# A state-space attention and MoE kernel: hand-ordered schedule replaced by a searched step list, with four operations moved to other engines

## The chip, the cores and the metric

The kernel runs on one core of one Trainium2 chip. The metric is the device time in microseconds (us) of one execution. A core has five engines that run their own instruction queues in order: TensorE (PE; its weight loads, PEld, overlap its matmuls), VectorE (DVE), ScalarE (ACT), GpSimd (POOL) and SyncE (SP), which here only issues transfers. Sixteen DMA engines move data between HBM and the on-chip memory.

## The reference, cut to what matters

```python
# attention, per batch b (4) and head h (8), 768 steps, head size 48
for t in range(S):
    cur = einsum('bhd,bhe->bhde', u * k[t], v[t])
    y[t] = einsum('bhd,bhde->bhe', r[t], state + cur)
    state = w[t][..., None] * state + einsum('bhd,bhe->bhde', k[t], v[t])
x = y.transpose(0, 2, 1, 3).reshape(3072, 384)      # tokens x (heads * size)
out = gelu_tanh(x @ w_in) @ w_out                   # 384 -> 2048 -> 384
```

Both kernels cut the tokens into 12 units: three windows of 256 tokens for each of four batches. A unit goes through attention (decay sums `z`, `x`; scaled operands `kk`, `rq`; their transposes `T`; scores `mt`; output `y`; state product `p`), then a transpose of its 256x384 result, then the MoE part: `h` (48 matmuls), GELU `g`, and `o` (32 matmuls).

## The kernel before

Weights arrive as fp32 on SyncE's queue and three engines convert them. Operand transposes are on PE for the first three units and on the DMA after that. Scores are masked by a product; the `u` diagonal is added apart.

```python
def load_w_in(i):
    t = pstage.tile([P, DF // 2], FP, tag=f"wi{i}", name=f"wi{i}")
    SP.dma_start(out=t, in_=moe_w_in[ts(cb, P), ts(hf, DF // 2)])
def cast_w_in(i, eng):
    cast(eng, w_in_sb[:, cb, ts(hf, DF // 2)], stages.pop(("i", i)))
...
PE_T = (3, 3)
def a2(q, which):
    if q < PE_T[which]:                       # units 0 to 2: PE, then a copy by VectorE
        ...
        return
    for c2 in range(2):                       # units 3 to 11: two DMA transposes
        SP.dma_start(out=..., in_=src[...], transpose=True)
...
    a6(0)                                     # x of unit 0 is ready
    cast_w_in(0, ACT)
    cast_w_in(1, ACT)
    att = attention(1)
    ...
    table("gelu")
    for i in range(8):
        mm1(0, i)                             # all of h of unit 0
        if i in (0, 2, 4, 5, 6, 7):
            next(att)                         # attention of unit 1 in between
    table("exp")                              # only now: decays of unit 2
    ww(2)
    ln(2)
    mm2(0, 0, range(6))
    a1(2)
    exps(2)
```

ScalarE loads a function table before it changes between logarithm or exponential on one side and GELU on the other (25 loads of 1.28 us in this trace).

## Time and profile before

| what | value |
|---|---|
| time, median of 3 (range) | 201.08 us (201.01 to 201.49) |
| PE busy in the profiled run | 179.5 of 202.0 us |

The profile's main lines are shown in the prediction.

### The profile page before, as it was taken

The page shows a single profiled execution, that of the slowest core. Times are in us where ns is not written, and L with a number is a line of the kernel's source. Part 1 is how long each engine was busy: PE and PEld are TensorE (multiplying, and loading weights), DVE is VectorE, ACT ScalarE, POOL GpSimd, SP SyncE. Part 2 cuts the span into 40 slices and gives each one's busy share as a digit, 9 for nine tenths or more (in the row PEclk, how much of TensorE's full clock was granted, in tenths as well). Part 3 has the DMA queues.
Part 4 walks back from the last instruction along what each step waited for, and adds up shares of the span by engine and source line. Part 5 has one row for each costly group of instructions (what it writes and reads, how often), then busy time and mean ns, then how long its engine had stood idle before and what let it go on. Part 6 is the DMA issues. An engine that isn't in the chain of part 4 may idle for free.

```text
span 202.0 us, 5310 instructions
## 1 busy us (share of the span) xinstructions
PE 179.5 (89%) x2200; PEld 126.4 (63%) x2200; DVE 132.7 (66%) x238; ACT 117.0 (58%) x188; POOL 124.3 (62%) x126
## 2 busy tenths in 40 slices
PE   3867499599998796999999999999989999999991
PEld 1245167485676564866767767677567677776760
DVE  7499874529888585548486697797397677374011
ACT  2226647876474483568585665674584757456650
POOL 3999683595985995895892993964967910000000
PEclk9998569999999999999999999999999999999997
DMA  6999999999559967878969959769879564301102
GB/s 160 258 270 334 394 301 332 221 272 251 142 80 211 242 121 177 208 99 198 225 119 251 156 95 259 151 134 279 121 169 209 92 118 69 80 3 35 46 9 68
DMA packets 76552, 35.15 MB, mean 174 GB/s; under 512 B 70512, under 2 KB 75760, under 8 KB 76528
## 3 DMA queue, kind: packets, MB, share of 16 engines
q1 hardware_dynamic: 76528, 34.81, 78.1%
q8 instruction: 17, 0.28, 0.7%
q14 instruction: 7, 0.06, 0.1%
HBM read 25.36 MB, written 4.72 MB: 149 GB/s over the span
## 4 chain that ended last, share of the span: by engine, by line
PE 58%; DMA 9%; DVE 4%; ACT 4%; SPq 3%; issue 2%; POOL 2%; ACTq 0%; POOLq 0%
PE h L393 24%; PE o L402 22%; DMA TT<-rq 7%; SPq L272 3%; PE mt L285 3%; PE y L308 2%; DMA TT<-kk 2%; PE cum L181 2%; PE y L356 2%; PE p L331 2%; PE xTp L378 1%; ACT L163 1%; DVE rq L244 1%; DVE kk L244 1%; POOL rk L206 1%
## 5 line engine op out<-in xcount | busy, mean ns | idle before, releaser
L395 ACT ACTIVATE g<-h 128x512 bf16<-128x512 f32 x96 | 56.8, 597 | 52.1 <-PE h L393 50.9
L393 PE MATMUL h<-xT,w_in_sb 128*128 128x256 bf16 x576 | 76.9, 277 | 5.2 <-DVE w_in_sb L86 2.2
L402 PE MATMUL o<-w_out_sb,g 128*128 128x384 bf16 x384 | 72.5, 326 | 0.5 <-DVE w_out_sb L86 0.5
L393 PEld LDWEIGHTS <-w_in_sb 128*128 128x128 bf16 x576 | 54.1, 99 | 18.5 <-issue 5.3
L402 PEld LDWEIGHTS <-g 128*128 128x128 bf16 x384 | 36.6, 98 | 18.8 <-issue 0.7
L291 DVE TENSOR_TENSOR mtsb<-mt,mask 128x512 bf16<-128x512 f32 x48 | 29.9, 683 | 5.3 <-PE mt L285 5.2
L216 POOL TENSOR_TENSOR vsc<-vb,dg 128x768 bf16<-128x768 bf16 x12 | 17.9, 1490 | 9.9 <-DVE dg L215 7.3
L215 DVE TENSOR_REDUCE dg<-rk 128x16 f32<-128x768 f32 x12 | 11.4, 948 | 17.7 <-POOL rk L206 17.7
L410 DVE COPY ob<-o 128x384 f32<-128x384 f32 x24 | 13.2, 551 | 14.2 <-PE o L402 13.8
L206 POOL TENSOR_TENSOR rk<-rk,r 128x768 f32<-128x768 f32 x12 | 21.7, 1809 | 0.9
L202 POOL TENSOR_TENSOR rk<-k,u_bc 128x768 f32<-128x768 f32 x12 | 21.7, 1812 | 0.1
L256 POOL TENSOR_TENSOR am<-blk,al 128x384 f32<-128x384 bf16 x24 | 20.2, 860 | 0.0
L163 ACT ACT_TABLE_LOAD x13 | 16.7, 1283 | 0.9 <-PEq L645 0.7
L194 POOL TENSOR_TENSOR kw<-k,w 128x384 f32<-128x384 f32 x9 | 9.0, 999 | 12.7 <-DMA k<-in_k_dram 12.7
L345 DVE TENSOR_TENSOR p<-p,S 128x384 f32<-128x384 f32 x16 | 9.1, 567 | 9.9 <-PE p L331 9.1
L165 ACT ACT_TABLE_LOAD x12 | 15.4, 1283 | 0.2
L168 ACT ACTIVATE logw<-ww 128x384 bf16<-128x384 f32 x12 | 6.2, 523 | 14.8 <-POOL ww L173 10.4
L195 POOL TENSOR_TENSOR rw<-r,w 128x384 f32<-128x384 f32 x10 | 10.3, 1032 | 5.7 <-DMA r<-in_r_dram 5.7
L364 DVE TENSOR_TENSOR xs<-y,vsc 64x384 bf16<-64x384 f32 x24 | 13.3, 554 | 0.7
L285 PE MATMUL mt<-TT,TT 48*64 48x128 bf16 x384 | 10.1, 227 | 3.3 <-DMA TT<-rq 2.4
L346 DVE TENSOR_TENSOR S<-p,am 128x384 bf16<-128x384 f32 x20 | 11.1, 557 | 2.6 <-PE p L331 1.9
L285 PEld LDWEIGHTS <-TT 48*64 48x64 bf16 x384 | 6.8, 110 | 7.4 <-issue 7.2
(68 smaller groups left out, 189.6 us busy)
## 6 DMA issues: line engine op xcount, KB each, us to landing
w<-in_w_dram SPq DMA_DIRECT2D x12, 384.0 KB, 6.1
k<-in_k_dram SPq DMA_DIRECT2D x12, 384.0 KB, 5.4
r<-in_r_dram SPq DMA_DIRECT2D x12, 384.0 KB, 5.8
v<-in_v_dram SPq DMA_DIRECT2D x12, 384.0 KB, 6.5
out_dram<-ob SPq DMA_DIRECT2D x48, 96.0 KB, 2.3
wi<-in_moe_w_in_dram SPq DMA_DIRECT2D x6, 512.0 KB, 8.8
wo<-in_moe_w_out_dram SPq DMA_DIRECT2D x8, 384.0 KB, 5.8
TT<-kk SPq DMA_TRANSPOSE x18, 3.6
```

The lines of the kernel that those rows point to most:

```text
L163: ACT.preload_act_table_set(EXP_SET)
L165: ACT.preload_act_table(AF.Gelu_apprx_tanh)
L202: POOL.tensor_tensor(out=rk, in0=kt.rearrange("p h (t d) -> p h t d", t=2), in1=u_bc[:, :, None, :].broadcast_to([P, H, 2, D]), op=AL.mult)
L206: POOL.tensor_tensor(out=rk, in0=rk, in1=rt.rearrange("p h (t d) -> p h t d", t=2), op=AL.mult)
L216: POOL.tensor_tensor(out=vsc, in0=vb, in1=dg.rearrange("p h t -> p t h")[:, :, :, None].broadcast_to([P, 2, H, D]), op=AL.mult)
L256: POOL.tensor_tensor(out=st["am", q][:, c2], in0=blk.rearrange("p g j d -> p g (j d)"), in1=st["al", q][:, :, c2][:, :, None].broadcast_to ...
L285: PE.matmul(mts[j][ds(64 * c2, 64), gi, t2, :], kT[ds(64 * j, D), c2, g, t2, :], rT[ds(64 * j, D), c2, g, :, :], start=(gi + t2 == 0), sto ...
L291: DVE.tensor_tensor(out=sb[:, j], in0=mts[j], in1=mask.rearrange("p a b t -> p a (b t)")[:, None, :, :].broadcast_to([P, 2, 2, P]), op=AL. ...
L364: DVE.tensor_tensor(out=st["xs", q][rows, c2, :].rearrange("p (h d) -> p h d", h=H), in0=ys[c2][rows, :, :], in1=st["vsc", q][ds(64 * c2, ...
L393: PE.matmul(h[:, f, :], w_in_sb[:, cb, ts(ft, P)], xT[:, :, cb, :], start=(f + cb == 0), stop=(cb == NCB - 1), skip_group_check=True)
L395: ACT.activation(out=st["g", q][:, ds(2 * i, 2), :], in_=h, func=AF.Gelu_apprx_tanh)
L402: PE.matmul(st["o", q, c2], g[:, ft, ts(c2, P)], w_out_sb[:, ft, :], start=(ft == 0), stop=(ft == NFT - 1))
```

## The change

The intent is to keep PE full. A list of some 1,000 steps, found by search, fixes the order on every engine and the PSUM bank of every result. With it come these parts (core of the diff, cuts marked "..."):

```diff
+ORDER = """
+const.3.D load.w.0.0 const.2.D load_u.A clr.sc.2.P clr.lwl.0.D load.w.0.1 clr.rq.1.P lnL.0.0
+...
+cum.2@7 Xc.0.A sel.1 a5.1.1 xd.2@1 clr.lw.1.P xs.1.0.A ez.2 xs.1.1.A mm1.0.3@3 sm.0.1
+..."""
-        SP.dma_start(out=t, in_=moe_w_in[ts(cb, P), ts(hf, DF // 2)])
-        cast(eng, w_in_sb[:, cb, ts(hf, DF // 2)], stages.pop(("i", i)))
+        POOL.dma_start(out=w_in_sb[i],                       # fp32 to bf16 on the way
+                       in_=moe_w_in[:, ts(i, sz)].rearrange("(c p) f -> p c f", p=P))
...
-            DVE.tensor_tensor(out=sb[:, j], in0=mts[j], in1=mask..., op=AL.mult)
+        POOL.tensor_tensor(out=<diagonal of sc>, in0=eye..., in1=d..., op=AL.mult)     # dI
+        DVE.copy_predicated(sc..., mask..., st["mt", q, n][j]...)                      # mk
...
-        for dst, tri in ((x, strict), (z, incl)):
-            PE.matmul(dst[:, 0:HD], tri, lw[:, :, 0:D], start=True, stop=True)
+        PE.matmul(z[:, 0:HD], incl, lw[:, :, 0:D], start=True, stop=True)
+        DVE.tensor_tensor(out=x..., in0=z..., in1=logws[q % NLW][:, :, 0:D], op=AL.subtract)
...
-            PE.transpose(ps[:, c2, cb, :], xs[:, c2, ts(cb, P)], ident)   # all units
+        SP.dma_start(out=st["xT", q][:, c2], in_=..., transpose=True)     # Xd, units 6 to 11
...
+            ACT.activation(out=t.rearrange("p f (c i s) -> p (f c) s i", c=2, s=2),
+                           in_=h.rearrange("p f (c s i) -> p (f c) s i", c=2, s=2),
+                           func=AF.Gelu_apprx_tanh)                       # for those units
...
-            POOL.tensor_tensor(out=st["am", q][:, c2], in0=blk..., in1=al..., op=AL.mult)
+    (state updates read the decay directly, in halves of 64 partitions, on VectorE)
```

Operand transposes stay on PE for units 0 to 4 and for one operand of unit 5. In the step list, `mm1.0.3@3` is chunk 3 of `h` of unit 0 into bank 3, and a last letter names the engine. Attention of units 0 and 1 now comes before any `h`, and 44 small dummy matmuls (`warm`) stand in the gaps.

## The prediction

> **What bounds the kernel now.** I read the page's busy shares and slices first, then the costliest groups, then the chain of work that ended last, then the busy times of the first 50 us in stretches of 5 us.
>
> ```profile
> span 202.0 us, 5310 instructions
> PE 179.5 (89%) x2200; PEld 126.4 (63%) x2200; DVE 132.7 (66%) x238; ACT 117.0 (58%) x188; POOL 124.3 (62%) x126
> ...
> PE   3867499599998796999999999999989999999991
> PEclk9998569999999999999999999999999999999997
> DMA  6999999999559967878969959769879564301102
> ```
>
> TensorE is the fullest engine, and the other three have a third of the span free. But the tenth-filled slices show two regimes: nine slices of start-up (45 us) with holes and a dip of the clock, then a nearly full PE.
>
> ```profile
> 160.84 1.31 PE h L393 x12
> 162.15 0.57 PE mt L285 x32
> ...
> 165.31 0.51 PE y L308 x32
> 165.81 0.34 PE p L331 x8
> ...
> 170.19 0.34 PE xTp L378 x6
> 170.52 3.25 PE o L402 x20
> 173.77 1.31 PE h L393 x12
> ```
>
> This is the chain (start, length, what) over one undisturbed unit (one of 12 windows of 256 tokens): 173.77 - 160.84 = 12.93 us, all PE. It gives the true cost of each kind of matmul when they follow one another, which the group means (277 ns for `h`) hide because those overlap: `h` (first MoE product) 1.31/12 = 0.109 us each, 48 a unit, 5.25 us; `o` (second product) 3.25/20 = 0.1625, 32 a unit, 5.20 us; scores `mt` 0.57; `y` 0.51; `p` 0.34; from other rows of the same chain the state product 0.17 for each half (0.34), the x transposes 0.34, the decay sums 0.40 (0.33 for the two of 384 columns), 16 kk/rq transposes 0.89 (0.445 for one operand), four diagonal matmuls (`sel`) 0.33.
>
> Useful PE work before: 12 x (5.25 + 5.20 + 0.57 + 0.51 + 0.34 + 0.34) = 146.5, less 4 x 0.17 = 0.7 for the state products that four first halves don't have, plus transposes of x 4.1, sums 4.8, 6 operand transposes 2.7, `sel` for six units 2.0: **159.4 us**. So 202.0 - 159.4 = 42.6 us of the span is not useful PE work. It splits so: at 40.21 us the PE has done about 14.9 us of it (units 0 and 1 of attention, one unit and a quarter of `h`, eight `o`): 25.3 us lost. From 40.2 to the last matmul's end at 197.6 us there are 157.4 us for the remaining 144.5: 12.9 lost. From there the last eviction and store take 4.4.
>
> ```profile
> 20.00:25.00 5.00, 2.05 (x12) 1.00 (x10) 4.54 (x5) 3.69 (x4) 3.50 (x2) 0.50 1.02 403
> 35.00:40.00 5.00, 3.03 (x24) 1.94 (x23) 2.84 (x7) 4.25 (x7) 2.25 (x3) 1.00 0.93 223
> ```
>
> (PE, PEld, DVE, ACT, POOL busy, granted clock, DMA share, GB/s.) MoE starts at 20.4 us but gets no further: PE is 2.05 of 5 us busy at half clock, waiting for weights that VectorE, ScalarE and GpSimd convert (2.3, 1.06 and 1.5 us for 128x1024). At 35 to 40 us it waits for converted output weights, tables and gelu. The later loss is mostly this:
>
> ```profile
> 58.77 0.57 SPq L272
> 59.39 2.84 DMA TT<-rq
> ```
>
> a DMA transpose of the scores' operand, issued behind other DMAs, with the PE waiting.
>
> **What the Trainium skill says.** "TensorE: Matmul & The Clock Gate", Part 1 (the HAM clock gate): a PE idle over a window of about 3.4 us drops to half clock, and a busy window restores it. The trace agrees roughly: after 10 to 20 us at 70% modelled busy with gaps, the clock is 0.50 and 0.60 in the two next stretches. "DMA: Bandwidth & Descriptors", SWDGE vs HWDGE vs iDMA: a cast during DMA needs GpSimd's software descriptors, so the new weight loads must be issued from there. The kernel before has none; no run shows its rate yet. The same page, Queues, rings and completion order: each DMA engine goes round its queues by packet, so GpSimd's weights will share with SP's inputs instead of standing behind them. The trace before has nearly everything on one queue, so doesn't show it. "TensorE: Matmul & The Clock Gate", Weight-path perf modes: fast weight load wants 128 columns, not fp32, with a column step of -1,023 to 1,024 elements; the new step of 4 is inside. No weight load before is strided, so the trace doesn't show this either.
>
> **The change part by part.**
>
> *Weights.* The six `wi` and eight `wo` loads with staging, and 14 casts (6 for w_in 8.5 us, 8 for w_out 5.3 us over three engines) go. Six converting DMAs take their place. Off the steady path, on the start-up path. Bytes read don't change: 12 x 1.57 MB inputs and 6.3 MB weights. Inputs ran at 209 GB/s in the first 10 us, weights at up to 403. Two units of inputs (3.15 MB) cost about 15 us of DMA, all weights 16, two more units 15: 48 us with the 2 us of first landing, against PE's need of all of it at about 50 us. Tight, but no wall.
>
> *Order.* Attention of units 0 and 1 now goes side by side before any MoE; then `h` of both units (10.5 us of matmul in a row), and only then `o`. Following the step list with before's durations: w lands at 5 to 6 us, logarithms, sums and exponentials until about 9; k and r with them until 14 (six VectorE products of 0.55); transposes, copies and first scores at 13.5; v late because it is loaded seventh, about 16.5; unit 0's masks 18.2, unit 1's masks, dg and vsc until 22.3 on VectorE in order; y of unit 1 22.9, x transposes and a ScalarE copy of 0.85: first `h` at **24.3 us**. That is 4 later than before, but PE has by then done 9.5 us of useful work and has two whole units in front of it.
>
> *PE work.* The strict decay sum of ten units becomes a VectorE subtraction: -10 x 0.165 = -1.7. The first two units take seven 384-column matmuls instead of two: +1.7. `sel` for four units goes, since the diagonal is written into the score matrix by GpSimd and masked scores are copied over it: -1.3. x transposes of six units go to DMA: -2.0. kk/rq transposes on PE rise from 6 to 11: +2.2. Broadcast of u: +0.7. Sum -0.4: **159.0 us**. The change saves almost no PE work; its gain is in the holes.
>
> *The other engines.* VectorE: 48 predicated copies, taken as today's masks (0.683) 32.8; kk/rq 48 x 0.547 = 26.3; subtractions 5.5; state updates now in halves of 64 partitions, 72 of about 0.36 (0.547 less 192 elements at the measured 1.06 ns each between the 384 and 512 forms) 25.5; dg 11.4; copies of T, xs, xT and ob about 18; clears 4: 123 against 132.7. ScalarE: gelu 57.3, 18 table loads instead of 25 23.1, exponentials and logarithms 22.5, copies 29: 132 against 117. GpSimd: rk 43.4, kw/rw/ww 30, diagonals 20 x 1.15 = 23 (from 0.86 for 384), the rest about 13 and unknown descriptor work: 110 to 120, `am` (20.2) and most of `vsc` (15) gone. None is over 75% of 180 us, so PE stays the bound.
>
> *Sum.* 24.3 + (159.0 - 9.5) = 173.8 for the last matmul if PE never stops. Tail 4.2 (the last piece is halved, its store's latency isn't). Losses: 2.5 for a half clock at the start of the dense part (few dummies, sparse PE from 10 to 24 us, as before), 1.5 for late weights, 3 in the steady part instead of 12.9, since waits for transposes shrink when five units use PE transposes and the order gives later ones more slack. Span 185.0; the timed runs lie 0.9 under the profiled span (201.08 against 202.0): **184.1 us**.
>
> **Rivals.** (1) The DMA is the bound of the first 50 us: software descriptors slower than 400 GB/s, or inputs starved by the weights. For it: DMA share 0.9 to 1.2 in nearly every early stretch before. Then first `h` at 28 or later and holes before the first `o`: 189 to 193. (2) Strided weight loads no longer hide behind the 0.109 us matmul: 576 times 20 ns, +11.5, so 195. Against it: the skill's range, and that `y` loads 128 columns in pairs every 0.03 us, a threefold margin. (3) Predicated copies cost twice a mask product: VectorE 156 us, its in-order queue then holds the scores and the evictions: about 191. (4) The search leaves no losses but tail and start: 177 to 178.
>
> **Range and chances.** Nearly 17 us of gain come from start-up, some 10 from waits; to lose both, rivals (1) and (2) would have to hold together. Half the uncertainty is the first `h` (22 to 28), half the steady losses (1 to 8): 178 to 191. Faster by over 2% (under 197.1) 0.95, same 0.04, slower 0.01.
>
> **What would show it right or wrong.** Right: `h` starting at 22 to 26 us and PE at 9 in all slices from there to the last but one; useful PE per unit still about 12.6 us; `h` at 0.109 us a matmul; no cast rows; landings of the weights before 35 us. Wrong: waits of PE on DMA for w_in or w_out of several us (rival 1), a larger `h` spacing (rival 2), masks over 1 us (rival 3), or PE waiting for the DMA-transposed x of units 6 to 11, which now stands between a unit's attention and its MoE and which I put at no cost.

## More of the kernel before

One more view is needed later: PE's waits (engine, operation and line, "<-", the releaser: us in total, times, longest).

```profile
PE mt L285 <- DMA TT<-rq: 2.4, 4, 1.0
PE h L393 <- DVE w_in_sb L86: 2.2, 1, 2.2
PE cum L181 <- ACT logw L168: 2.1, 4, 1.1
```

Scores wait for a DMA transpose, `h` for a converted weight, decay sums for a logarithm.

## The result, and the profile after

| | before | after |
|---|---|---|
| time, median (range), us | 201.29 (201.01 to 202.59), 4 runs | 181.28 (181.03 to 181.77), 4 runs |
| span of the profiled run, us | 202.0 | 179.2 |

The ratio of the times is 0.8987, with a 95% interval of 0.8944 to 0.9031. Ratios are the mean time of one kernel's runs over the mean of the other's in the same rounds, so they are not quite the ratio of the medians quoted. Executions over 1.5% slower than the fastest of the same kernel are left out of the means. The prediction was 184.1 us, in a range of 178 to 191: the time fell in the range, 2.8 us under the centre.

From the page of the kernel after, the span, the busy time of each engine, and the 40 slices:

```profile
span 179.2 us, 5484 instructions
PE 171.8 (96%) x2274; PEld 135.0 (75%) x2274; DVE 114.8 (64%) x241; ACT 125.3 (70%) x215; POOL 110.0 (61%) x115
...
PE   7999689999999999999999999999999999999993
PEclk9999999999999999999999999999999999999999
DMA  5999999999999999969999979869394312520244
```

The start-up with holes has shrunk to some five slices, and the dip of the clock is gone. The other engines have a quarter or more of the span free, as they had.

The chain of waits of the kernel after, where it enters the MoE part (start, length, what):

```profile
10.46 11.11 DMA w<-in_w_dram
...
21.64 1.00 POOL ww L324
...
22.66 0.53 ACT logw L328
...
23.24 0.32 PE z L367
...
24.34 1.31 PE h L626 x12
```

The first `h` waits for unit 2, not for its own operand: `w` of unit 2 lands at 21.6 us, GpSimd multiplies its even and odd steps, ScalarE takes the logarithm, and PE, which takes its queue in order, stands at the decay sum `z` ahead of `h`. (The first record of `h` starts at 24.18 us, overlapping the state product before it, which the chain counts first.) The interval of `h` is 1.31/12 = 0.109 us, as before.

The busy time of the kernel after by stretch (PE, PEld, DVE, ACT, POOL, then granted clock, DMA share, GB/s):

```profile
20.00:25.00 5.00, 3.14 (x62) 2.36 (x60) 3.71 (x10) 2.61 (x6) 2.62 (x4) 1.00 1.20 265
25.00:40.20 15.20, 15.20 (x209) 13.52 (x208) 10.28 (x21) 13.71 (x24) 12.89 (x13) 1.00 1.12 233
40.20:176.30 136.10, 135.88 (x1766) 107.92 (x1764) 86.23 (x174) 96.12 (x160) 77.42 (x66) 1.00 0.82 161
```

From the first `h` at 24.2 us to the last matmul's end at 176.3 us PE stops for 0.2 us in all (by the modelled ends of its matmuls). The DMA engines are full (mean share over 1.0 in each of these stretches up to 40 us). Before the first `h` PE waits 1.5 us for the logarithm behind the landing of `w`; after it, PE waits for no transfer.

The costliest groups of the kernel after, ScalarE's two GELU rows and VectorE's masked copy (busy, mean ns of one):

```profile
L634 ACT ACTIVATE g<-h 128x512 bf16<-128x512 f32 x48 | 33.2, 753 | 23.0 <-PE h L626 23.0
L638 ACT ACTIVATE g<-h 128x512 bf16<-128x512 f32 x48 | 26.1, 606 | 4.4 <-PE h L626 4.1
...
L519 DVE CAST_PREDICATED sc<-mask,mt 128x512 bf16<-128x512 uint16 x48 | 30.4, 686 | 9.9 <-PE mt L512 8.8 <-POOL rk L462 0.5 <-POOL sc L473 0.4
```

The GELU that also reorders columns (units 6 to 11) takes 753 ns against 606. The predicated copy takes 686 ns, the masking product before took 683.

**Where the 22.8 us of span came from.** At the first `h` (24.2 us) PE had done 9.5 us of useful work by the price list, so by 40.2 us it had done at most 9.5 + 16.0 = 25.5, against 14.9 before: 10.6 us. The dense part took 176.3 - 24.2 = 152.1 us for 159.0 - 9.5 = 149.5 of useful work: 2.6 lost against 12.9, so 10.3 us. The tail is 179.2 - 176.3 = 2.9 against 4.4: 1.5 us. The price list itself changed by 0.4. Sum: 22.8. The profiled run of before was one of its slower ones: later runs of it have spans of 199.3 and 200.8 us for times of 201.06 and 202.59. Hence the time fell by 20.0 us only.

### The profile page after: what moved, and what is told of

It reads as the page before. It is cut to its first block, busy times and chain, and to the rows that moved or that the text cites. A ratio compares the mean times of both kernels' runs of the same rounds, so it can differ in the third digit from the quotient of the medians.

```text
span 179.2 us, 5484 instructions
## 1 busy us (share of the span) xinstructions
PE 171.8 (96%) x2274; PEld 135.0 (75%) x2274; DVE 114.8 (64%) x241; ACT 125.3 (70%) x215; POOL 110.0 (61%) x115
## 3 DMA queue, kind: packets, MB, share of 16 engines
q10 hardware_dynamic: 1042, 1.28, 2.5%
## 4 chain that ended last, share of the span: by engine, by line
PE 79%; ACT 7%; DMA 6%; SPq 5%; POOL 1%; issue 0%
PE h L626 33%; PE o L652 33%; DMA w<-in_w_dram 6%; SPq L290 5%; PE mt L512 3%; ACT g L634 3%; PE y L534 2%; PE y L584 2%; PE T L433 2%; ACT L713 1%; ACT L711 1%; PE p L550 1%; PE Xp L601 1%; PE z L367 1%; ACT logw L328 1%; PE p L554 1%
## 5 line engine op out<-in xcount | busy, mean ns | idle before, releaser
L652 PE MATMUL o<-w_out_sb,g 128*128 128x384 bf16 (+1 forms) x400 | 73.4, 320 | 0.0
L626 PE MATMUL h<-xT,w_in_sb 128*128 128x256 bf16 x576 | 70.2, 273 | 0.2 <-ACT g L634 0.2
L626 PEld LDWEIGHTS <-w_in_sb 128*128 128x128 bf16 x576 | 62.2, 114 | 3.7
L652 PEld LDWEIGHTS <-g 128*128 128x128 bf16 x400 | 36.4, 98 | 16.5 <-ACT g L634 0.3
L519 DVE CAST_PREDICATED sc<-mask,mt 128x512 bf16<-128x512 uint16 x48 | 30.4, 686 | 9.9 <-PE mt L512 8.8
L473 POOL TENSOR_TENSOR sc<-eye,dg 128x512 bf16<-128x512 bf16 x20 | 20.6, 1042 | 5.9 <-DVE dg L467 5.9
L272 DVE COPY ob<-o 128x384 f32<-128x384 f32 (+1 forms) x12 | 6.3, 535 | 21.4 <-PE o L652 21.4
L575 DVE TENSOR_TENSOR s<-p,al 64x192 bf16<-64x192 f32 x40 | 14.1, 352 | 2.3 <-PE p L550 1.6
L593 DVE CAST xs<-y 128x384 bf16<-128x384 f32 x12 | 6.7, 556 | 13.7 <-PE y L584 13.7
L324 POOL TENSOR_TENSOR ww<-w 128x384 f32<-128x384 f32 x10 | 10.0, 1000 | 5.2 <-DMA w<-in_w_dram 3.6
L567 DVE TENSOR_TENSOR p<-p,s 64x192 f32<-64x192 f32 x32 | 11.7, 365 | 0.8
```

The source lines that it names most:

```text
L473: POOL.tensor_tensor(out=bass.AP(tensor=o.tensor, offset=o.offset, ap=[list(o.ap[0]), [256, 4], [192, 2], [1, 64]]), in0=eye[:, None, None ...
L519: DVE.copy_predicated(scs[q % NSC][n][:, :, j].rearrange("p a b c i -> p a (b c i)"), mask.rearrange("p a b t -> p (a b t)").bitcast(U16)[ ...
L567: DVE.tensor_tensor(out=p2[rows, :, pc], in0=p2[rows, :, pc], in1=s[rows, :, cols], op=AL.add)
L575: DVE.tensor_tensor(out=s[rows, :, cols], in0=p2[rows, :, pc], in1=st["al", q][rows, :, c2][:, :, None].broadcast_to([64, G, D]), op=AL.mult)
L626: PE.matmul(h[:, f, :], w_t, xt[:, :, cb, :], start=(f + cb == 0), stop=(cb == NCB - 1), skip_group_check=True)
L652: PE.matmul(st["o", q, c2], st["g", q, i][:, f, ts(m, P)], w_out_sb[i * NWO // 8][:, (2 * i + f) % (NFT // NWO), cols], start=(i + f == 0) ...
```

## The experiments

Two readings were to be told apart. **Theory A: the order.** Every part of the change is worth little alone; a part put into the old order moves the wait to the next late operand. **Rival B: the parts.** Weight conversion, late DMA transposes and a loaded GpSimd are the causes of the holes, and removing them, singly or together, gives most of the gain. All variants gave correct results. They ran on three chips; the variants of one share the runs of the kernel before, whose medians were 201.68, 201.91 and, over its fast runs, 202.02 us. The changed kernel was not run again. So a variant of it is compared with it through two ratios to before, each with an interval of some 0.4 to 0.6%, about 1 us: differences of that size are not clear of noise.

### b_conv: converting weight transfers in the old order

```diff
-    for i in range(6):
-        load_w_in(i)
...
+        POOL.dma_start(out=w_in_sb[i], in_=moe_w_in[:, ts(i, DF // 4)]...)   # 4, and 2 for w_out
-    cast_w_in(0, ACT)            # and the 13 other casts
```

> The kernel before with one part of the change alone: the weights come in six converting DMAs issued from GpSimd; the fourteen casts and the staging are gone, everything else keeps its order. If the start-up loss of the kernel before is mainly the conversion of the weights, the matmuls h of unit 0 are done by about 28 us instead of 36 and the time falls by 6 to 10 us, to 191 to 195. If it is mainly the order of the attention of units 0 and 1 and of the loads, h still waits or the time saved is lost again in the waits for scores: 198 to 201.

Measured: 202.37 us, ratio 1.0039 (0.9987 to 1.0092). No gain, and just above the second range. Busy time by stretch, a line of PE's waits, and its longest case in PE's timeline:

```profile
20.00:25.00 5.00, 4.71 (x40) 3.02 (x41) 4.00 (x8) 2.84 (x5) 4.98 (x6) 0.50 1.20 206
30.00:40.00 10.00, 7.48 (x105) 5.91 (x105) 4.47 (x9) 6.31 (x11) 4.39 (x6) 1.00 1.05 226
```

```profile
PE cum L190 <- ACT logw L177: 4.9, 4, 2.9
```

```profile
16.54 0.48 PE L190 MATMUL cum<-logw,strict 128*128 128x384 bf16 x1 [2.85 <-ACT logw L177]
```

PE is 4.71 of 5 us busy from 20 to 25, where it had been 2.05: the wait for weights is gone. The clock there is still 0.50. But the waits for logarithms grow from 2.1 to 4.9 us. Of these, 2.9 are for unit 1's, at 16.5 us (1.1 before): I had put two transfer issues, 1.7 us of GpSimd, ahead of `ww` of unit 1, which begins at 14.94 instead of 13.21 us. The first `h` comes at 23.5 us, where before had it at 20.4. The wait for unit 2's logarithm grows only from 0.4 to 1.0 us. The chain from 33 us on is two table loads of 1.28 us with unit 2's logarithm and exponentials between them, and it lets `h` go on at 40.7 us; in the profiled run of before that was 40.2 us. So the time saved on weights was lost before the first `h`, in part to the place that I gave the issues, and the table switches stood behind it as before. Another place for the issues in the old order was not tried.

### b_conv_tab: the same, with unit 2's decays ahead of the first GELU

```diff
+    ww(2)
+    ln(2)
+    a1(2, (1, 1))
+    exps(2)
     table("gelu")
...
-    table("exp")                 # and its decays, behind h of unit 0
```

> The kernel before with converting weight loads, and with the logarithm, sums and exponentials of unit 2 moved ahead of the first gelu, and its products ahead of the first o, as in the changed kernel. The converting loads alone gave nothing (202.4 against 201.7). If what held the PE between 35 and 41 us is the pair of table switches with the exponentials between gelu of unit 0 and of unit 1, about 5 us go: the first h of unit 1 after its gelu comes at 36 instead of 41 us, and the time falls to 195 to 198. If the start is held by the inputs, which are only now landing, the wait moves to the new place (gelu of unit 0 then stands behind w of unit 2), and the time stays at 200 to 203.

Measured: 207.7 us, ratio 1.0304 (1.0226 to 1.0382). Worse, and outside both ranges. Busy time by stretch:

```profile
25.00:30.00 5.00, 0.04 (x1) 0.04 (x1) 0.95 (x1) 0.52 (x1) 4.90 (x5) 0.50 1.14 232
```

Everything but GpSimd stands still. GpSimd's queue takes `ww` of unit 2 only at 28.35 us, behind `am`, `vsc`, `kw`, `rw` and `rk` products and two transfer issues, and PE stands 6.3 us for the logarithm. Moving one step earlier on ScalarE needs the same move on GpSimd.

### b_noam: the am products off GpSimd in the old order

```diff
-            POOL.tensor_tensor(out=st["am", q][:, c2], in0=blk..., in1=al..., op=AL.mult)
-        DVE.tensor_tensor(out=sn, in0=p2, in1=am[:, c2], op=AL.mult)
+            DVE.tensor_tensor(out=sn[rows, :, cols], in0=p2[rows, :, cols], in1=al..., op=AL.mult)
```

> The kernel before with one part alone: GpSimd no longer writes the 24 products am of the block mask and the decay (20.2 us); VectorE multiplies the diagonal blocks by the decay itself, in halves of 64 partitions, as in the changed kernel. If GpSimd, 75 to 100% busy from 50 to 160 us, is what makes rk, dg and with them the scores and the transposes late, the waits at 62 to 69 and 85 to 92 us shrink and the time falls by 2 to 5 us, to 196 to 199. If VectorE's place in the order is what they wait for, its own time grows by 24 x 0.15 us and nothing is gained: 200 to 203.

Measured: 202.97 us, ratio 1.0074 (1.0015 to 1.0132). Relief of GpSimd alone, with the work given to VectorE, gains nothing; the scores' wait for DMA transposes went from 2.4 to 3.2 us.

### b_peT: PE transposes for units 3 and 4 in the old order

```diff
-    PE_T = (3, 3)
+    PE_T = (5, 5)
```

> The kernel before with one other part alone: the scores' operands kk and rq of units 3 and 4 are transposed by the PE and evicted by VectorE, as the changed kernel does, instead of by DMA transposes. It adds 4 x 0.445 = 1.8 us of PE work. If the waits for DMA transposes at 59 and 75 us are what the steady part loses, 4 to 6 us of wait go and the time falls by 2 to 4 us, to 197 to 199. If the PE would have waited there anyway, for GpSimd's rk and the reduction behind it, the time stays at 200 to 203.

Measured: 206.63 us, ratio 1.024 (1.0175 to 1.0306). Slower (whether by more than 2% is unclear), and outside both ranges. PE's waits:

```profile
PE T L267 <- DVE kk L244: 5.4, 8, 2.4
```

The waits for DMA transposes (2.4 us before) are gone, but the PE transposes wait for VectorE's `kk` products, 5.4 us in place of 1.4. The longest wait, 2.4 us for unit 3, is a matter of place: `kk` comes no later than before (its first product begins at 53.92 us, at 54.29 before), but the transposes now stand ahead of 16 `o` matmuls in PE's queue. PE transposes put behind those were not tried.

### b_three: these three parts together in the old order

The edit is the sum of b_conv, b_noam and b_peT.

> The kernel before with three parts of the change together and its own order otherwise: weights in converting transfers from GpSimd, the am products off GpSimd, and PE transposes for units 3 and 4. Theory A (the order is the gain; parts put into the old order only move the wait): 198 to 208 us, no better than the parts alone (202.4, 203.0, 206.6). Theory B (the parts complete one another: converting weights free the queue and the engines early, the relief of GpSimd lets ww and rk come in time, PE transposes need no transfer): 188 to 196 us, at least a third of the 20 us gained. First h expected near 24 us under both; the theories differ in what TensorE does from 25 to 60 us: under A it is under 7 of 10 busy in two stretches of ten, under B above 9 of 10 in all.

Measured: 208.16 us, ratio 1.0274 (1.0218 to 1.0331), just above the range of Theory A. The parts do not complete one another. PE's waits, and one stretch:

```profile
PE T L274 <- DVE kk L256: 5.4, 8, 3.0
```

```profile
50.00:60.00 10.00, 6.85 (x80) 4.30 (x80) 6.37 (x14) 1.48 (x4) 5.14 (x4) 0.66 0.73 166
```

PE is 6.85 of 10 busy at 50 to 60 us, with no engine full and the clock down to 0.66. It is the only stretch under 7 of 10; Theory A had named two, Theory B none (30 to 40 us has 7.38). First `h` was at 23.6 us, as expected under both theories. Rival B falls for these three parts in the places given to them: they gave nothing, alone or together, in the old order. The other parts of the change were not tried there.

### a_Td: DMA transposes for units 2 to 4 in the new order

```diff
-T.2.0@7 ... Tc.2.0.A ... T.2.1@1 ... Tc.2.1.D      # and units 3, 4
+Td.2.0 ... Td.2.1
```

> The changed kernel with DMA transposes for the scores' operands of units 2 to 4 again, as the kernel before has from unit 3: 6 x 0.445 = 2.7 us of PE work less, six copies less on VectorE and ScalarE. If the PE transposes are what keeps the dense part free of waits, as I predicted, the PE then waits two to four times for some 2 us, and the time is 182 to 187. If the order has enough slack in itself, it falls to 178.5 to 180.

Measured: 200.87 us, ratio 0.9971 (0.9911 to 1.0031): the whole gain is lost, far outside both ranges. Busy time by stretch, and PE's waits:

```profile
35.00:40.00 5.00, 0.00 (x0) 0.00 (x0) 0.00 (x0) 0.00 (x0) 2.49 (x2) 0.63 1.09 232
```

```profile
PE mt L506 <- DMA T<-rq: 14.1, 2, 13.4
```

One wait of 13.4 us holds four engines, and the clock falls too. A load of `k` stood at SyncE's head from 30.6 us for 6.9 us (it does in the changed kernel as well), so the transposes were issued at 37.6 and 43.0 us and landed near 47. Why that load took so long is not shown: the DMA engines were full (share 1.1), and GpSimd had issued an output weight at 27.1 and at 30.7 us. In this list the PE transposes of the early units are essential, because DMA transposes stand behind SyncE's input loads. Whether a list searched anew could place DMA transposes there was not tried.

### a_cast: weights by SyncE and engine casts in the new order

```diff
-load_win.1 (a converting transfer from GpSimd; also 0, 3, 2 and two of w_out)
+load.v.1 load_win.1 ... xs.0.1.A cw.1.A ... Xc.0.A cw.0.A   # fp32 on SyncE, then a cast
```

> The changed kernel with its order, but weights loaded as fp32 on SyncE's queue after the inputs that stood there, and cast by the engines in ten instructions of 0.7 to 3 us each. Theory A (in the new order the weight route is of little weight, as it was in the old one): within 2 us of the changed kernel, 180 to 184 us. Theory B (the converting route is needed in the new order, since SyncE's queue already holds input loads back 6.9 us and three engines are busy 60 to 70 per cent): 188 to 198 us, with first h at 30 us or later and TensorE waiting for casts or for inputs of units 3 and 4 up to 60 us.

Measured: 185.07 us, ratio 0.9125 (0.9073 to 0.9177), that is 2.8 us (by the ratios: 0.0138 of 202) to 3.8 us (by the medians) above the changed kernel. Neither theory's range held it. (There are eight casts, not ten.) Busy time by stretch, and PE's waits:

```profile
25.00:30.00 5.00, 4.06 (x41) 3.76 (x42) 3.29 (x7) 4.97 (x10) 0.94 (x1) 1.00 1.03 270
30.00:40.00 10.00, 8.21 (x105) 7.75 (x103) 6.75 (x13) 7.21 (x15) 5.91 (x6) 1.00 1.08 342
```

```profile
PE mt L516 <- DVE T L446: 1.8, 1, 1.8
```

First `h` is at 24.0 us, as in the changed kernel. The loss follows, from 25 to 50 us, where casts stand ahead of attention work on ScalarE and VectorE and an output weight lands only at 42.7 us. Taking the converting route out of the new list costs some 3 us; putting it into the old order gained nothing. In this run 17 of the 20 us remain without it.

### a_nodummy: no dummy matmuls

```diff
-warm.16@0 ... warm.1@2 ... warm.2@3 ... warm.3@2 ... (44 matmuls)
```

> The changed kernel without any dummy matmul (48 of 256 columns gone). My prediction counted 2.5 us for a half clock at the start of the dense part, which the trace does not show: the clock stays at 1.00. If the dummies are what held it, the granted clock falls to about 0.5 for some microseconds between 5 and 30 us, and the time rises by 1.5 to 4 us, to 183 to 185. If the real matmuls alone were enough, the clock stays and the time is 181.0 to 181.6.

Measured: 182.59 us, ratio 0.9049 (0.9005 to 0.9093): 1.3 us above the changed kernel, between the two ranges. The intervals of the two ratios overlap; but the four runs (182.11 to 183.28) all lie above those of `a_h_first` (180.76 to 181.67). Busy time by stretch in the profiled run:

```profile
20.00:25.00 5.00, 4.82 (x62) 2.90 (x62) 4.48 (x11) 2.46 (x5) 5.00 (x7) 0.50 1.20 269
25.00:30.00 5.00, 5.00 (x43) 4.37 (x42) 3.05 (x7) 3.75 (x8) 4.98 (x6) 0.74 1.20 264
```

Without dummies the clock is 0.50 as the dense part begins. One of the four runs had a mean clock of 1.00 and still took 182.34 us, so the half clock is not shown to be all of the 1.3 us.

### a_h_first: unit 2's decays behind the first h

```diff
-ln.2 sa.0.1 ... cum.2@7 Xc.0.A sel.1 a5.1.1 xd.2@1 ... ez.2 xs.1.1.A mm1.0.3@3
+sa.0.1 ... Xc.0.A sel.1 a5.1.1 ln.2 ... xs.1.1.A mm1.0.3@3 cum.2@7 xd.2@1 ez.2
```

> The changed kernel with the work of unit 2 that waits for its w (logarithm, decay sums, their exponentials) moved behind the x transposes of unit 0 and the first h, so that the first h no longer stands behind a load that landed at 21.6 us. If that wait is worth what the chain says, the first h starts at 22.4 us instead of 24.2 and the time falls by 1.0 to 1.8 us. If gelu, which cannot start before the exponentials of unit 2 have used the other table, is the real gate, h runs out of PSUM banks after four groups, and the time changes by less than 0.5 us.

Measured: 181.02 us, ratio 0.8973 (0.8933 to 0.9014): not told from the changed kernel, as in the second case, though by another gate than the one named there. The chain:

```profile
22.77 0.81 PE h L620 x6
...
25.31 1.47 PE h L620 x12
```

`h` starts 1.4 us sooner, but has only twelve matmuls done by 24.5 us, with unit 2's sums between them. It goes on at 25.3 us, behind VectorE's subtraction and state updates for units 2 and 0.

### a_start: one weight transfer issued later, so that unit 2's w comes sooner

```diff
-load_win.0 dg.0 ... rkb.1.P ... load_win.3         # issue between the rk products
+dg.0 ... rkb.1.P ... load_win.0 load_win.3         # issue behind them
-mm1.0.0@2 ... mm1.0.2@5
+mm1.0.2@2 ... mm1.0.0@5                            # needs that weight later
```

> An attempt to be faster than both: the changed kernel with the first weight transfer's issue put off behind the two early rk products, [...]and the first three h groups taken in an order that needs that weight later; the logarithm of unit 2 goes before the copy of x. Theory A (first h, and so the end, hangs on the landing of w of unit 2 at 21.6 us): w lands by 20.5 us and the time falls 0.7 to 1.5 us, 179.8 to 180.6. Theory B (the GELU and exponentials that follow are the gate, as the run with unit 2's work behind the first h suggested): within 0.4 us of the changed kernel.

Measured in five rounds: 181.81 us (181.09 to 182.93), ratio 0.8978 (0.8931 to 0.9025). No gain: by the medians 0.5 us more, by the ratios 0.2 less. The timeline of GpSimd:

```profile
17.16 1.57 POOL L302 DMA_DIRECT2D w_in_sb<-in_moe_w_in_dram  x2
18.76 2.93 POOL L485 TENSOR_TENSOR vsc<-vb,dg 128x768 bf16<-128x768 bf16 x2
21.65 0.99 POOL L319 TENSOR_TENSOR ww<-w 128x384 f32<-128x384 f32 x1
```

`ww` of unit 2 now waits for no transfer, yet begins at 21.65 instead of 21.64 us: the issue that I moved takes 0.8 us of GpSimd, and it now stands ahead of `vsc` and `ww` in that queue. Later, `w` of unit 4 lands at 40.0 us and PE waits for its logarithm. No tried version beats the changed kernel.

### a_X: x transposes of units 6 to 11 back on PE

```diff
-Xd.6.0 ... Xd.6.1
+X.6.0@1 X.6.1 Xc.6.D        # and 7 to 11; plain GELU
```

> The changed kernel with the transposes of x back on PE for units 6 to 11 (36 transposes more, copied out by VectorE, plain GELU). My price list: 36 transposes of some 0.055 us are 2.0 us of PE; GELU falls from 753 to about 600 ns on 48 instructions, 7.2 us of ScalarE. Theory A (TensorE is the bound from 24 us on, and ScalarE's longer GELU is hidden): +1.5 to +2.5 us, 182.8 to 183.8. Theory B (the longer GELU held TensorE as much as the transposes cost): within 0.5 us of the changed kernel, 180.8 to 181.8.

Measured: 185.79 us, ratio 0.9169 (0.9109 to 0.9228): 3.7 us (by the ratios) to 4.5 us (by the medians) more. Both theories missed. PE's waits:

```profile
PE mt L507 <- DVE xT L604: 0.6, 1, 0.6
PE y L529 <- DVE xT L604: 0.5, 1, 0.5
```

PE's busy time, with its modelled ends, grew by 175.1 - 171.8 = 3.3 us, more than the 2.0 of the price list. The rest is new waits, these two among them, for copies by VectorE that the list was not searched for. ScalarE lost 5.8 us of work (119.5 against 125.3), and it was worth nothing: the longer GELU had been hidden.

### a_str: the reordering done by h's moving operand instead of the GELU

```diff
+                if q in by_dma:
+                    rhs = rhs.rearrange("p c (s i) -> p c i s", s=2)
-            ACT.activation(out=<reordered>, in_=<reordered>, func=AF.Gelu_apprx_tanh)
+        ACT.activation(out=t, in_=h, func=AF.Gelu_apprx_tanh)
```

> The changed kernel, units 6 to 11: h reads the DMA-transposed x in the order of the tokens (moving operand with a step of 64 elements) so that gelu reads and writes in one run; before, gelu wrote every second element and took 753 ns instead of 606. If a strided moving operand costs the PE nothing, h stays at 0.109 us a matmul, gelu falls to about 600 ns (7 us of ScalarE less), and the time falls by 0.5 to 2 us, since ScalarE stands on the chain at 110 to 122 us. If the PE streams strided columns slower, 288 matmuls lose 20 ns or more each and the time rises by 6 us or more.

Measured: 218.92 us, ratio 1.087 (1.0802 to 1.0939). GELU is back at 602 ns, and PE pays. All records of `h` (ns min/median/max):

```profile
L624 PE MATMUL h<-xT,w_in_sb x576: 272/352/432, 23.6 to 207.9; 128*128 128x256 bf16 x192
```

Busy time of `h` rose from 70.2 to 108.8 us. Only half of the 576 matmuls read strided: 38.6/288 = 0.134 us each, beside 0.109 for the plain one. Neighbouring columns now lie 64 elements (128 bytes) apart. The Trainium skill, "SBUF — State Buffer", Door 1: The DMA port swizzle, says that accesses run at full rate while at least two fall in one 16-byte line, which for bf16 bounds a free stride to 8 elements. The case agrees for the step of 64, which more than doubles the matmul. A step of 4, which the page would have free, is not quite: the strided weight load takes 114 ns, the plain one of the kernel before 99 (115 in `b_conv`, where the step stands in the old order). It is hidden, since the interval of `h` stayed at 0.109 us.

## Why the prediction was right, and where not

The time was right, and so was the main step: the gain lies in the holes of PE, not in PE's work. That the centre came within 2.8 us is partly luck, since two errors of opposite sign met (see the span, below). By its own steps:

- **"first `h` at 24.3 us".** Measured 24.18. The number held, the cause did not. The walk through VectorE's masks put the operand of `h` last. In fact the operand was there some 1.4 us earlier (a_h_first starts `h` at 22.77), and unit 2's logarithm was the gate. Part of the agreement is luck.
- **"Weights" as the start-up loss.** "PE is 2.05 of 5 us busy at half clock, waiting for weights": a correct reading of a wait, but not shown to be the cause of the loss. b_conv removes the wait and gains nothing: in part the place of its issues delayed unit 1's decays, and the table switches around unit 2's decays stood behind it as before. In the kernel after, the last weight landed near 40 us (issue at 31.4 us, 8 to 9 us to landing), not "before 35 us" as the list of signs has it, and PE did not wait for it.
- **"The later loss is mostly this ... a DMA transpose".** The wait is real but mis-sized: PE's waits for these transposes sum to 2.4 us, of 157.4 - 151.5 = 5.9 us that PE stands from 40.2 us on. b_peT is 4.9 us slower without them for two units, since PE then met `kk` too early in its queue.
- **"2.5 for a half clock".** Measured 0: the clock is 1.00 from 0 to 176 us in the profiled run. I took 44 small dummies for too few. With them the clock held; without them it fell in three of four runs, and 1.3 us were lost. The prediction's "agrees roughly" is too kind for the idle window of some 3.4 us that it cites: in the kernel before the clock fell from about 18 us on, although PE's longest gap from 8 to 20 us was 1.1 us. What sets the clock is not shown here.
- **"1.5 for late weights" and "3 in the steady part".** Together 4.5 against 2.6 lost in the dense part. PE never waited for a weight. The direction was right, the size somewhat large.
- **"Tail 4.2".** Measured 2.9. The halved last piece and its quicker store were under-rated by 1.3 us.
- **The span and the offset.** The sum gave a span of 185.0, 5.8 above the measured 179.2: 2.5 + 1.9 + 1.3 from the three points above, and 0.1 from the first `h`. Against this, "the timed runs lie 0.9 under the profiled span" had the wrong sign. In each run the time is 1.7 to 2.1 us over its span (181.13 for 179.2). I had compared different executions. This error of some 2.8 us hid half of the other.
- **"Nearly 17 us of gain come from start-up, some 10 from waits".** This sentence contradicts the sum above it, which gives 17.0 us in all: 25.3 - (14.8 + 4.0) = 6.5 in start-up, 9.9 in the steady part, 0.2 in the tail and 0.4 of PE work. Measured were 10.6, 10.3, 1.5 and, unmeasured by itself, 0.4.
- **"x transposes of six units go to DMA: -2.0".** Probably mis-sized: undoing it costs 3.7 to 4.5 us (a_X), of which 3.3 are PE's busy time. The list was not searched for the undone version, so the transposes' own share is not separated.
- **The engines.** VectorE 114.8 (said 123), ScalarE 125.3 (said 132), GpSimd 110.0 (said 110 to 120). The GELU's reordering, 48 x 0.147 = 7 us, was not priced; it is hidden.
- **The rivals.** (1) DMA as the bound: not in this order, although the engines are full to 40 us. In a_Td six pairs of transposes more on SyncE's queue cost 19.6 us; whether the full DMA engines or that queue held them back is not separated. (2) Strided weight loads: a load takes 114 ns where it took 99, but `h` keeps its 0.109 us. (3) Predicated copies: 686 ns, so no. (4) No losses but start and tail, 177 to 178: the nearest to the trace, since the dense part lost 2.6 us only.

What is shown is that three of the parts, in the places given to them, gain nothing in the old order, and that removing parts from the new one costs 1.3 (dummies), some 3 (weights), some 4 (x transposes) and 19.6 us (early PE transposes). These do not add up, since each removal also upsets a list searched for it. That the order by itself makes the gain is argued from this: the old operations all together in the new order were not run, because the list is written for the new ones; nor were the masked copies, the subtraction or the x transposes by DMA run in the old order, nor better places for the parts that were. The clock is a smaller rival left open: in the kernel before it was 0.88, 0.50 and 0.60 in the stretches from 15 to 30 us. An estimate from PE's busy time there (0.12 x 3.81 + 0.50 x 2.05 + 0.40 x 5.00) puts its cost at up to 3.5 of the 20 us; dummies alone in the old order were not tried.

## What to carry to other kernels

A wait in the profile names the operand that came last, not the one that would come next: before pricing its removal, follow the in-order queue of every engine to the second-latest operand. When several engines are each two thirds busy and the fullest one has holes, suspect the order of the queues: here single repairs only moved the holes, in part because of where in the queues they were put. Before trading a hidden cost on a free engine for a tidy access pattern, ask what that pattern does to the engine that bounds.

## What the Trainium skill lacked or had wrong

- No rate for a predicated copy was found ("VectorE: DVE Perf Modes"): 128x512 fp32 from PSUM to bf16 took 686 ns, as much as the masking product (683).
- "SBUF — State Buffer" states a penalty for strides without a size, has a step of 4 bf16 elements free, and "TensorE: Matmul & The Clock Gate" doesn't apply it to the moving operand: with a step of 64 bf16 elements, 0.134 us more for 256 columns, on 0.109. A strided weight load (step 4) shows 114 ns against 99, which is hidden.
- "DMA: Bandwidth & Descriptors" gives software descriptors a fixed first-byte cost, but not the time they hold GpSimd's queue: 0.76 to 0.93 us for each converting transfer here, enough to undo a reordering (a_start). Nor does it give how long the issue of a plain load can hold SyncE's queue: 6.9 us at 30 to 37 us here, with a DMA share of 1.1 (cause not shown; the transposes of a_Td stood behind it).
- "ScalarE: Activation LUTs" has no cost for a reordering access: the GELU of 128x512 with reordered columns took 753 ns against 606.
- No page has the cost of GpSimd writing the diagonals of 64x64 blocks: 1042 ns for one score tile of 128x512.
